# First batch's row products of the two halves in own PSUM banks, joined by VectorE; transfer lengths of the planner changed

## The chip, the cores and the metric

The kernel runs on one core of a Trainium2 chip. A core has five engines, each with its own instruction queue that is worked off strictly in order: TensorE (PE, matrix products into PSUM), VectorE (DVE), ScalarE (ACT), GpSimd (POOL) and SyncE (SP, here only a queue for transfers). 16 DMA engines move data between DRAM and SBUF for the queues of SP, ACT and POOL. The metric is the time of one execution in microseconds (us), as the device measures it; lower is better.

## The reference: what is computed

Two stages follow each other, for 4 batches of 768 positions. The first is attention in chunks: 8 heads of 64, each chunk of 32 positions sees 16 positions to the left, 8 to the right and 8 memory rows.

```python
for c in range(nc):                       # 24 chunks of 32
    k_full = np.concatenate([mem_k, k_ctx], axis=2)
    scores = scale * np.matmul(q_c, k_full.transpose(0, 1, 3, 2))
    a = softmax(scores)
    out[:, :, c_start:c_end] = np.matmul(a, v_full)
```

The result, as x of 4 x 768 x 512, goes through a Fourier mix and a two-layer network:

```python
X = np.fft.fft(np.fft.fft(x, axis=1), axis=2)
u = x + np.real(X)
un = (u - mean(u)) / np.sqrt(var(u) + 1e-06)
out = u + np.maximum(un @ w_ch1, 0.0) @ w_ch2      # 512 -> 2048 -> 512
```

## The kernel before

**Attention.** The 8 heads of a batch are taken in 4 pairs; over the whole run the pairs are numbered 0 to 15 (batch 0 has 0 to 3, batch 1 has 4 to 7). Per pair, `e_load_q` and `e_load_k` (L310, L315) issue a q and a k transfer on POOL, which also turn the numbers into bf16. `e_load_v` (L320) issues six transfers on SP into a buffer `va`; `e_overlap` (L339) copies on POOL, once per head, 32 rows of `va` to the rows where neighbouring chunks overlap. `e_turn_q`, `e_turn_k` transpose on PE, `e_qT` and `e_kT` copy the result out of PSUM, `e_scores` and `e_exp` make the weights for one half (group g) of the sequence, `e_values` (L430) multiplies them with `va` on PE, and `e_norm` (L443) divides on DVE. There are 4 buffers each for q and k, 3 for `va`.

**Fourier mix.** The real part of the two-dimensional transform is computed as cosine and sine products. The columns are folded first (`pq`, `ff`), so that sums and differences of mirrored columns remain. Each folded block is split into two fp16 parts, `hi` (ACT, L501) and `lo` (DVE, L506). The row products (`row_products`, L509) multiply these on PE with the tables `cosS` and `sinS` of the sequence axis, 12 matrix products of 128x193 for one result; a result is named by `par` (even or odd output columns) and `ab` (0 for cosine, 1 for sine). Each is split again into `up` (cast on ACT, L528) and its rest (DVE, L532), reversed into `dn` (DVE, L537), and goes as the left operand into the column products on PE.

**Batch 0 in its own form.** To begin before all of batch 0's attention is there, its columns are folded in two halves h = 0 (pairs 0 and 1) and h = 1 (pairs 2 and 3), with `e0_pq` (L554), `e0_ff` (L587) and `e0_ff_edge`. `e0_rows` (L597) accumulates both halves into the same four PSUM banks `ps0`, one for each (par, ab): first the four results of h = 0, later the four of h = 1 on top. Where par and ab differ, h = 1 enters with a minus sign, which a negated table gives (`e_neg`, L782, on DVE). `e0_edge` (L571) adds the products of one boundary column, 24 of one row, whose parts POOL prepares in `e0_edge_parts` (L562).

**The network.** `unT` (512 x 768 per batch, transposed, fp16) goes through the first layer (`e_ch1`, L666, 4 products of 128x384 per group, `relu` on ACT into `hT`) and the second (`e_ch2`, L679, from `hT`). The weights are fetched by POOL with conversion to fp16: `load_w1` (L889) and `load_w2` (L899), four transfers each. The buffer of w2 is the one that held v of pair 3 (`last`), so that w2 is issued after the values of pair 3.

**The order.** All of this is written as tasks with an engine, a cost, predecessors, buffers to take and give, and for transfers a length `moved`. `Plan.order` (L59) plays them through with these numbers and hands out the order in which each engine's instructions are written, and the PSUM bank of each result. The numbers are estimates in the source; only the order follows from them, and on the chip each engine waits where data is not there. `wire` in the planner sums the lengths of all transfers one behind the other:

```python
if t["moved"] and e == "POOL":
    beside = max(beside, now + cost) + 1.15 * t["moved"]
    wire = max(wire, now + cost) + t["moved"]
    t["done"] = beside + self.LAG["DMA"]
```

Where PE has nothing to do in the plan, filler products (`e_warm`, six at a time) are put in. POOL's transfers use eight semaphores in turn: each waits for the one eight before it on POOL to have landed.

The softmax here doesn't subtract the row's maximum and nothing guards it: scores larger than these inputs give would overflow.

## Time and profile before

| | us |
|---|---|
| median of 13 runs (304.32 to 309.48) | 305.77 |
| the profiled execution | 305.29 |
| its span, first to last instruction | 303.4 |
| PE busy | 290.1 (3333 products) |
| DVE busy | 179.5 |
| ACT busy | 166.1 |
| POOL busy | 72.4 |
| row products of batch 0, h = 1 (48 products) on PE | about 40.4 to 44.4 from the start |
| first product of the first layer | 54.9 from the start |

The busy time of an engine is the time in which one of its instructions runs; an idle stretch is followed in the trace by the instruction that ended it and by what released it (`<-`). The chain of waits is followed back from the last instruction to whatever released each step. In timelines, the first number is the start from the beginning of the span, the second the duration; `x12` means twelve instructions in one entry. SPq and POOLq are the queue parts of these engines. The granted clock of TensorE is 1.00 at full speed.

### The profile page before, as it was taken

What the parts mean: (1) busy time and instruction counts of PE and PEld (TensorE: products, weight loads), DVE (VectorE), ACT (ScalarE), POOL (GpSimd) and SP (SyncE); (2) the same over time, 40 slices, a digit from 0 to 9 for tenths busy, and PEclk for the clock granted to TensorE, in tenths of its full rate; (3) what the DMA queues carried; (4) which work ended last, traced back from release to release, by engine and by line L of the source; (5) the groups of instructions that cost most, each with busy time, mean ns of one, the idle gap of its engine ahead of it and who ended that gap; (6) DMA issues with size and microseconds to landing.
All of it is one profiled execution on the core that took longest, in us unless ns stands there. A gap on an engine that the chain in (4) does not pass through costs nothing.

```text
span 303.4 us, 7854 instructions
## 1 busy us (share of the span) xinstructions
PE 290.1 (96%) x3333; PEld 193.1 (64%) x3333; DVE 179.5 (59%) x362; ACT 166.1 (55%) x297; POOL 72.4 (24%) x121
## 2 busy tenths in 40 slices
PE   8798998899999999999899999999999999999995
PEld 8677997556556666767566856656764554554644
DVE  7988967903323999789997889865931001002002
ACT  8967546686467757367655454721680450630710
POOL 7557732633235822025400020000020000000000
PEclk9999999999999999999999999999999999999999
DMA  6999999995995513213200001001000101101001
GB/s 80 158 165 191 195 202 194 197 190 69 189 175 95 106 30 96 67 31 99 56 0 2 35 37 38 0 37 52 19 0 35 72 0 69 37 0 69 37 35 69
DMA packets 42313, 24.49 MB, mean 81 GB/s; under 512 B 30375, under 2 KB 38823, under 8 KB 42279
## 3 DMA queue, kind: packets, MB, share of 16 engines
q0 software_dynamic: 9344, 10.49, 22.2%
q1 hardware_dynamic: 29479, 7.34, 13.6%
q10 hardware_dynamic: 3456, 6.16, 5.4%
q8 instruction: 26, 0.43, 0.6%
q14 instruction: 8, 0.07, 0.1%
HBM read 28.11 MB, written 6.29 MB: 113 GB/s over the span
## 4 chain that ended last, share of the span: by engine, by line
PE 74%; DVE 11%; DMA 7%; ACT 4%; POOL 2%; issue 1%; ACTq 0%; POOLq 0%; SPq 0%
PE pc L683 25%; PE ph L669 24%; PE xa L439 6%; PE pm L548 5%; DMA w_sb<-in_moe_w_ch_dram 5%; PE ps L513 4%; PE sc L384 2%; PE tp L648 2%; PE trq L348 2%; DVE xsb L450 1%; PE trk L363 1%; ACT e L427 1%; DMA qf<-in_q_dram 1%; PE pc_half L691 1%; DVE ff L490 1%
## 5 line engine op out<-in xcount | busy, mean ns | idle before, releaser
L676 ACT ACTIVATE hT<-ph 128x384 f16<-128x384 f32 x128 | 61.7, 492 | 58.9 <-PE ph L669 58.0
L669 PE MATMUL ph<-unT,w_sb 128*128 128x384 f16 x512 | 88.9, 326 | 1.9 <-ACT hT L676 1.6
L683 PE MATMUL pc<-w_sb,hT 128*128 128x512 f16 x368 | 85.7, 380 | 0.2 <-DVE osb L711 0.2
L669 PEld LDWEIGHTS <-w_sb 128*128 128x128 f16 x512 | 48.5, 98 | 34.5 <-issue 3.1
L711 DVE SCALAR_TENSOR_TENSOR osb<-pc,rstd,xsb 128x512 f32<-128x512 f32 x23 | 17.3, 751 | 74.8 <-PE pc L683 74.8
L683 PEld LDWEIGHTS <-hT 128*128 128x128 f16 x368 | 34.0, 98 | 37.1 <-issue 0.2
L341 POOL COPY va<-va 32x780 f32<-32x780 f32 x30 | 31.3, 1065 | 32.7 <-DMA va<-in_v_dram 20.8
L392 ACT ACTIVATE e<-sc,mbias 128x384 f32<-128x384 f32 x48 | 25.3, 581 | 13.4 <-PE sc L384 7.3
L439 PE MATMUL xa<-va,e 128*64 128x65 f32 x720 | 26.4, 225 | 2.2 <-POOL va L341 2.2
L439 PEld LDWEIGHTS xa<-va,e 128*64 128x64 f32 x720 | 23.1, 137 | 7.7 <-issue 3.4
L642 ACT ACTIVATE un<-xsb,mu_s 128x512 f16<-128x512 f32 x18 | 12.9, 719 | 14.6 <-DVE mu_s L636 13.8
L660 POOL TENSOR_SCALAR rstd<-mu_s 128x6 f32<-128x6 f32 x4 | 1.0, 245 | 77.8 <-DVE mu_s L636 77.7
L528 ACT CAST up<-ps 128x386 f16<-128x386 f32 x16 | 9.7, 605 | 17.7 <-PE ps L513 17.6
L450 DVE TENSOR_TENSOR xsb<-xa,zs 128x384 f32<-128x384 f32 x32 | 17.8, 557 | 1.1
L635 DVE BATCH_NORM_STATS2 st<-xsb 128x6 f32<-128x512 f32 x24 | 16.6, 690 | 0.6
L373 ACT COPY kTb<-trk 128x832 bf16<-128x832 bf16 x16 | 13.5, 854 | 3.6 <-PE trk L363 3.6
L353 ACT COPY qT<-trq 128x768 bf16<-128x768 bf16 x14 | 11.2, 798 | 7.2 <-PE trq L348 4.0
L506 DVE TENSOR_TENSOR lo<-ff,hi 128x768 f16<-128x768 f32 x14 | 14.4, 1043 | 0.9 <-ACT hi L501 0.9
L312 POOL DMA_DIRECT2D qf<-in_q_dram x16 | 10.5, 659 | 17.1 <-PE trq L348 11.7
L449 DVE RECIPROCAL zs<-xa 128x6 f32<-128x6 f32 x32 | 6.0, 188 | 13.6 <-PE xa L439 13.2
L317 POOL DMA_DIRECT2D kf_all<-in_k_dram x16 | 10.1, 632 | 15.2 <-PE trk L363 5.2
L368 DVE COPY kTb<-mkT 128x96 bf16<-128x96 bf16 x16 | 5.8, 388 | 12.8 <-PE sc L384 12.8
(147 smaller groups left out, 416.0 us busy)
## 6 DMA issues: line engine op xcount, KB each, us to landing
out_dram<-osb ACTq DMA_DIRECT2D x23, 256.0 KB
va<-in_v_dram SPq DMA_DIRECT2D x30, 176.0 KB
w_sb<-in_moe_w_ch_dram POOLq DMA_DIRECT2D x8, 512.0 KB, 12.6
qf<-in_q_dram POOLq DMA_DIRECT2D x16, 192.0 KB, 4.8
kf_all<-in_k_dram POOLq DMA_DIRECT2D x16, 192.0 KB, 5.7
va<-in_mem_v_dram SPq DMA_DIRECT2D x30, 24.0 KB
va<-in_v_dram SPq DMA_DIRECT2D x15, 28.0 KB
last<-in_v_dram SPq DMA_DIRECT2D x2, 176.0 KB
```

The lines of the kernel that those rows point to most:

```text
L341: nc.gpsimd.tensor_copy(v1[0:32, 1:NB, 0:D + 1], v1[96:128, 0:NT, 0:D + 1])
L373: nc.scalar.copy(strided(kTb[n % NKT], 0, [[BS, NB], [8, 8], [1, RB]]), strided(tr_of.pop((n, 1)), 0, [[8, NB], [1, 8], [KP, RB]]))
L392: nc.scalar.activation(e1[:, :, :, ts(half, 32)], sc[:, :, 0:6, ts(half, 32)], AFT.Exp, bias=mbias[:, half:half + 1], scale=1.0 / math.sqr ...
L439: nc.tensor.matmul(xa[64 * half:64 * half + 64, st, hh, 0:65], e1[:, hh, t6, :], v1[:, 6 * g + t6 + 1, 0:65], start=True, stop=True)
L450: nc.vector.tensor_tensor(xs[b][:, 3 * g:3 * g + 3, 2 * pr * D:(2 * pr + 2) * D] .rearrange("p s (h d) -> p s h d", h=2), xa[:, :, :, 0:D] ...
L506: nc.vector.tensor_tensor(lo[:, ab].rearrange(fl), ff_of[b, par][:, ab].rearrange(fl), hi[:, ab].rearrange(fl), ALU.subtract)
L548: nc.tensor.matmul(pm[:, par, :], lhs, rhs[:, par, :], start=(im == 0), stop=(im == 3))
L635: nc.vector.bn_stats(st6, xs[b][:, kt, :])
L669: nc.tensor.matmul(ph[:, 0:384], w1_sb[:, dt, ts(ht, P)], unT_of[b][:, dt, sh * 384:(sh + 1) * 384], start=(dt == 0), stop=(dt == NDT - 1))
L676: nc.scalar.activation(hT_of[b, sh][:, ht, :], ph_of.pop((b, sh, ht))[:, 0:384], AFT.Relu, bias=0.0, scale=-1.0)
L683: nc.tensor.matmul(pc_of[b, sh, stl], hT_of[b, sh][:, ht, ts(stl, P)], w2_of[0][:, ht, :], start=(ht == 0), stop=(ht == NHT - 1))
L711: nc.vector.scalar_tensor_tensor(osb, pc_of.pop((b, sh, stl)), rstd_of[b][:, st:st + 1], xs[b][:, st, :], ALU.mult, ALU.add)
```

## The change

Batch 0's two halves no longer share PSUM banks. For h = 0, three results are formed, each in a bank of its own: one for the cosine (both parities have the same one) and one per parity for the sine, since the edge products, which now open their own accumulation in row 0, differ there. For h = 1, two results are formed. So 5 times 12 products stand where 8 times 12 stood, and the negated tables go. ACT copies the three results of h = 0 to SBUF in float32 (`e0_keep`); DVE adds or subtracts the result of h = 1 (`e0_join`), four times; the cast (`e0_up`) and the rest (`e0_rest`) then read SBUF. The order of two predecessors changes with it: the edge parts follow the first `pq` of h = 1, and the second norm of pair 2 follows the `ff` of h = 0.

The planner's lengths change: v of batches 1 to 3 counts 0.9 instead of 1.6, each part of w1 2.2 instead of 3.2, each part of w2 2.2 instead of 3.5.

```diff
@@ e0_edge
-            row_products(ps_of[0, par, 1][0:1],
-                         [e128[:, i].unsqueeze(3) for i in range(2)], par, tab, 0, 1,
-                         False, False)
+            row_products(ps_of["own", par, 1][0:1],
+                         [e128[:, i].unsqueeze(3) for i in range(2)], par, tab, 0, 1)
@@
-    def e0_rows(par, ab, h):
-        if h == 0:
-            ps_of[0, par, ab] = bank([P, 2, NK], FP32, "ps0")
-        ps = ps_of[0, par, ab]
-        turned = h == 1 and par != ab
-        tab = neg_of[0][:, ab] if turned else (cosS if ab == 0 else sinS)
-        row_products(ps, hl_of[0, h], ab, tab, 0, P, h == 0, h == 1)
+    def e0_rows(key, ab, h):
+        ps_of[key] = ps = bank([P, 2, NK], FP32, "ps0")
+        row_products(ps, hl_of[0, h], ab, cosS if ab == 0 else sinS, 0, P)
+    t_of = []
+    def e0_keep(key, ab):
+        if not t_of:
+            t_of.append(fpool.tile([P, 2, 2, 2, NK], FP32, tag="unT", bufs=2, name="join"))
+        nc.scalar.copy(t_of[0][:, ab, key[1]], ps_of.pop(key))
+    def e0_join(par, ab):
+        op = ALU.add if par == ab else ALU.subtract
+        nc.vector.tensor_tensor(t_of[0][:, ab, par], t_of[0][:, ab, ab and par],
+                                ps_of["other", ab], op)
+    def e0_up(par, ab):
+        up = fpool.tile([P, 2, NK, 2], FP16, tag="up", bufs=4, name="up")
+        up_of[0, par, ab] = [up.rearrange("p i k s -> p i (k s)"), None, up]
+        nc.scalar.copy(up[:, 0].rearrange("p k s -> p s k"), t_of[0][:, ab, par])
+    def e0_rest(par, ab):
+        up = up_of[0, par, ab][2]
+        nc.vector.tensor_tensor(up[:, 1].rearrange("p k s -> p s k"), t_of[0][:, ab, par],
+                                up[:, 0].rearrange("p k s -> p s k"), ALU.subtract)
@@
-    def e_neg(i):
...
-    t_neg = [add("DVE", 0.4, lambda i=i: e_neg(i), t_sines[:2], rank=140 + i,
-                 take=("unT",) if i == 0 else ()) for i in range(2)]
@@ attention
-                  take=("va",) if hh == 0 and n != HP - 1 else (), moved=1.6) for hh in range(2)]
+                  take=("va",) if hh == 0 and n != HP - 1 else (), moved=1.6 if n < HP else 0.9) for hh in range(2)]
...
-                 [t_mkT, kept.get("mk"), t_clear["kTb", n] if n < NKT else None], take=("kTb",),
+                 [t_mkT, kept.get("mk"), t_clear["kTb", n] if n < NKT else None,
+                  kept["f0"] if n == HP + 1 else None], take=("kTb",),
@@ load_w1, load_w2
-            w1_sb[:, dt, :], moe_w_ch1[ts(dt, P), :]), [after], moved=3.2, rank=-1)
+            w1_sb[:, dt, :], moe_w_ch1[ts(dt, P), :]), [after], moved=2.2, rank=-1)
-        return [add("POOL", 0.7, lambda g=g: e_w2(g), [after], moved=3.5, rank=-1)
+        return [add("POOL", 0.7, lambda g=g: e_w2(g), [after], moved=2.2, rank=-1)
@@ part_of_first
-                ed = add("POOL", 0.8, e0_edge_parts, [pq[-1]], rank=-3)
-                ed = add("PE", 1.94, e0_edge, [ed, rows[0, 1], rows[1, 1]])
+                ed = add("POOL", 0.8, e0_edge_parts, [pq[1]], rank=-3)
+                ed = add("PE", 1.94, e0_edge, [ed, rows["own", 0, 1], rows["own", 1, 1]])
+                for par in range(2):
+                    own = rows["own", par, 1]
+                    keep[par, 1] = add("ACT", 0.6, lambda par=par: e0_keep(("own", par, 1), 1),
+                                       [ed], give=(("acc", own),))
...
+                more = [kept["tk0"]] + t_sines if h == 0 else []
+                for par in range(2 if (h, ab) == (0, 1) else 1):
+                    key = ("own", par, ab) if h == 0 else ("other", ab)
...
+            if h == 0:
+                keep[0, 0] = add("ACT", 0.6, lambda: e0_keep(("own", 0, 0), 0), [rows["own", 0, 0]],
+                                 take=("unT",), give=(("acc", rows["own", 0, 0]),))
+                t_norm[2, 1]["after"].append(ff)
+        join = up = None
+        for ab in range(2):
+            other = rows["other", ab]
+            for par in (1 - ab, ab):
+                t_join[par, ab] = join = add(
+                    "DVE", 0.6, lambda par=par, ab=ab: e0_join(par, ab),
+                    [keep[ab and par, ab], other, join],
+                    give=(("acc", other),) if par == ab else ())
+        for ab in range(2):
+            for par in (1 - ab, ab):
+                up = add("ACT", 0.5, lambda par=par, ab=ab: e0_up(par, ab), [t_join[par, ab], up],
+                         take=("up",))
+                t_rest[par, ab] = add("DVE", 0.45, lambda par=par, ab=ab: e0_rest(par, ab), [up],
+                                      give=("unT",) if par and ab else ())
```

## The prediction

> **What bounds the kernel now.** I read the busy table first. All times are us from the start of the profiled span.

> ```profile
> PE 290.1 (96%) x3333; PEld 193.1 (64%) x3333; DVE 179.5 (59%) x362; ACT 166.1 (55%) x297; POOL 72.4 (24%) x121
> ```

> TensorE (PE) is busy for 96% of the span, so the end is set by how much real work PE has left once it runs without a break, and by when that stretch starts. Windows of 5 us show where the break is:

> ```profile
> 45.00:50.00 5.00, 5.00 (x59) 4.30 (x58) 3.97 (x13) 3.45 (x6) 0.76 (x2) 1.00 1.22 196
> 50.00:55.00 5.00, 3.21 (x82) 2.66 (x80) 4.39 (x15) 1.74 (x4) 3.11 (x5) 1.00 1.22 196
> 55.00:60.00 5.00, 4.45 (x51) 2.83 (x52) 4.76 (x15) 4.16 (x8) 2.27 (x4) 1.00 1.22 197
> ```

> The columns are PE, weight loads, VectorE (DVE), ScalarE (ACT), GpSimd (POOL), granted clock, DMA share, GB/s. PE stands 1.79 us in the second window while the DMA engines move 196 GB/s. The chain of waits over 30 to 62 us says why:

> ```profile
> 35.98 15.31 DMA w_sb<-in_moe_w_ch_dram
> ...
> 51.88 0.14 POOL kf_all L317
> 52.02 0.50 issue
> 52.52 1.62 POOL va L341 x2
> 54.14 0.04 issue
> 54.18 0.80 PE xa L439 x20
> ```

> Nothing that PE, DVE or ACT does between 36 and 51 us is on it. The second w2 transfer lands at 35.98 + 15.31 = 51.29; then POOL issues a k load, then copies the overlap rows of v for pair 4 (the first of batch 1), and PE's attention values of pair 4 wait for that copy. POOL's timeline shows the queue that ties them:

> ```profile
> 35.19 3.04 POOL L897 DMA_DIRECT2D w_sb<-in_moe_w_ch_dram  x4
> 38.18 0.69 POOL L312 DMA_DIRECT2D qf<-in_q_dram  x1
> ...
> 48.44 0.63 POOL L312 DMA_DIRECT2D qf<-in_q_dram  x1 [3.31 <-DMA w_sb<-in_moe_w_ch_dram]
> 51.85 0.63 POOL L317 DMA_DIRECT2D kf_all<-in_k_dram  x1 [2.78 <-DMA va<-in_v_dram]
> 52.52 3.17 POOL L341 COPY va<-va 32x780 f32<-32x780 f32 x4
> 55.65 0.63 POOL L312 DMA_DIRECT2D qf<-in_q_dram  x1
> 58.42 0.63 POOL L317 DMA_DIRECT2D kf_all<-in_k_dram  x1 [2.15 <-PE tp L648]
> ```

> In the program each POOL transfer waits for the semaphore of the eighth POOL transfer before it. Counting back eight, the q load at 48.44 waits for w2 part 0, the k load at 51.85 for part 1 (landed 51.29, 0.56 earlier), the q load at 55.65 for part 2, the k load at 58.42 for part 3. The transfer view has part 3 landing 20.4 us after its start:

> ```profile
> w_sb<-in_moe_w_ch_dram POOLq DMA_DIRECT2D x1, 512.0 KB, 20.4
> ```

> The four issues at 35.19 take 3.04, so part 3 starts at about 37.45 and lands at 57.85; again 0.57 passes before the POOL instruction at 58.42. So the release label that names `tp` on that line is not the cause; the landing is.

> **The change, part by part.**

> Moved, and the term that decides. With shorter lengths (w1 and w2 2.2 instead of 3.2 and 3.5, v 0.9 instead of 1.6) the planner writes another order. On POOL the q and k loads of pair 9 now stand ahead of the four overlap copies of pairs 4 and 5; before, they stood behind. They are the two that wait for w2 parts 2 and 3. The bytes, the rings and the issue order up to there are the same, and the DMA engines carry 196 to 198 GB/s through this stretch, so I let part 3 land at 57.85 as before. Then the copies start not at 52.52 but after the k load: 58.42 + 0.63 + 0.04 = 59.09, which is 6.57 later. The values of pair 4, group 0 ended at 54.98 and now end at 61.55. Behind the two waiting loads stand six overlap copies, a q and a k load and batch 0's `rstd`; behind the waiting values on PE stands everything to the end.

> PE's order also changed: ahead of these values it now has the scores of pair 5 (0.27), two first-layer groups (2 x 0.65, from 10.40 for 16) and one turn of `un` (0.33). That is 1.90 done in the wait: 6.57 - 1.90 = +4.67. In the old order PE ran from 54.98 to 59.53 with 4.55 us for three first-layer groups (1.95), one values group (0.71) and three turns (0.9), so 0.99 went to waits on ACT's `hT`. Behind a 5 us stand all this is ready, so I take it back whole: +3.68. Bounds: w2 up to 0.5 earlier (the edge parts that precede its issue on POOL may come 0.5 sooner) or 0.5 later; the 0.99 regained from nothing to all.

> Removed: 36 row products (60 + 24 against 96 + 24). Twelve take 1.01, so 3.03 of PE. The two negated tables, 0.45 + 1.09 of DVE at 14.8, lie beside DMA and ACT; the first norm waits no longer for DVE, but the second still waits for PE.

> Added: three ACT copies from PSUM (0.60 each, from the `up` cast of the same 386 columns), four DVE sums and differences (0.56 to 0.60, from `pq` and the old rest); four `up` casts and rests now read SBUF (bounds 0.45 to 0.60). Walked on these rows: The last norm of pair 2 moves behind `ff`, which makes the second half's low parts 0.75 later, and the last row product ends at 42.3 instead of 44.4. Joins then run to 43.7 on DVE, casts to 44.6 on ACT, rests to 45.9 on DVE. Two of the ACT copies wait for the edge products (39.75); behind them on ACT stand the copy of q for pair 5, the four casts and the next `exp`. Behind the joins on DVE stand the rests, the reversals and batch 0's sums. The first column product starts at 45.1 (before 44.48) behind two scores and turns and four fillers of 0.51, the columns end at 52.9 (before 50.5), and PE reaches the values of pair 4 at about 54.8. It meets a copy that ends at 59.92. So the whole row-product part is costed at nothing: 5.1 us of standing hides it. If that cover were gone, the values would end at 55.65 against 54.98 with 1.90 more done: 0.67 - 1.90 = -1.2.

> The v lengths move the later pairs' attention forward in the order. PE stands there little: 50 - 48.13 = 1.87 between 100 and 150 us and 0.55 between 150 and 200. So this part lies between -2.4 (all of it gone) and +2.4 (as much again); I take 0, since the same engines remain busy and DMA is at 69 GB/s or less.

> Sum: 305.29 (the profiled run: span 303.4 and 1.89 around it) + 3.7 = 309.0. That run lies 0.48 under the median of 305.77, so against the median: 309.4.

> [...] This trace's w2 parts land 51.29 and, two later, 57.85: 3.28 us each. [...]

> The clock: the page's rows grant 1.00 throughout, over standing times up to 1.79 us; no row here shows PE standing 5 us. [...]

> **The rivals.**

> Faster (0.11): w2 part 3 lands early enough that the copies are no obstacle. Against it: 3.28 us each at a saturated 196 GB/s. Price -1.2, so 304.6; it needs the landing 3.7 us sooner than 57.85, at 54.2, just to break even.

> Paid back later (0.10): the stand occurs, but attention moved forward fills the 2.42 us of later standing and some waits of ACT's `hT` (1.6 in the waits) go too: 3.7 - 2.4 - 1.0 = +0.3, about 306.1. For it: the order is denser in attention after 62 us. Against: those waits come from short dependences that any order has.

> A second stand (0.09): the overlap copy for pair 6 waits for v, which landed before 65.36 in the old trace; the loads of pair 10 stand behind it. If PE's values of pair 6 or the turns of pairs 7 and 8 caught up with that, as much again as 3.7 would be lost: 313.1. Against it: PE has some 15 us of other work between.

> The change does not shorten (a rival to the gain only): joins and rests take longer than the two rows saved, and the columns start late. This I expect, but it is hidden.

> **How the numbers follow.** The likeliest (0.70) is the stand, 309.4, with its own range 306.5 to 313.3 from -0.5 -2.4 and +0.5 +1.0 +2.4. Dropping the faster case below and the top of the second stand above leaves about 8 in 10 in 305.0 to 312.8. A measurement tells 0.2% (0.6 us) from no change. Faster: 0.11 and a third of the paid-back case, 0.14; within: a third of it and the low end of the likeliest, 0.06; slower: the rest, 0.80.

> **What would show it.** Right: the overlap copies of pair 4 start near 59 on POOL, behind two loads that wait for `w_sb`; PE waits about 5 us for `va` before the values at about 55; the row products number 84 + later batches, and the four joins run near 41.3 to 43.7. Also to be seen: whether the clock stays 1.00 after it. Wrong: the copies start before 55.5, or PE arrives at the values later than 59, or standing time after 100 us goes away by over 2 us.

## The result and the profile after

The changed kernel takes 310.38 us (median of 11 runs, 308.98 to 311.62), the kernel before 305.89 (48 runs, 304.24 to 309.62). The ratio is 1.0143, 95% interval 1.0119 to 1.0167: slower by about 4.4 us. The forecast was 309.4, slower.

| us | before | after |
|---|---|---|
| the profiled execution | 305.29 | 311.26 |
| its span | 303.4 | 309.3 |
| PE busy | 290.1 | 290.3 |
| PE not busy, 0 to 30 | 5.13 | 6.19 |
| PE not busy, 30 to 56 | 1.83 | 1.98 |
| PE not busy, 56 to 100 | 0.51 | 5.34 |
| PE not busy, 100 to 200 | 2.42 | 2.12 |

The span grew by 5.9, PE's idle time by 5.7 (19.0 against 13.3), and 4.83 of that lies between 56 and 100 us. The busy table of after and its windows of 5 us (columns as before) show the place:

```profile
PE 290.3 (94%) x3327; PEld 193.9 (63%) x3327; DVE 177.4 (57%) x364; ACT 167.7 (54%) x300; POOL 68.7 (22%) x121
```

```profile
50.00:55.00 5.00, 5.00 (x65) 4.30 (x63) 3.97 (x15) 2.99 (x5) 1.26 (x2) 1.00 1.22 197
55.00:60.00 5.00, 2.09 (x26) 1.24 (x24) 4.79 (x16) 4.19 (x8) 0.63 (x1) 1.00 1.23 199
60.00:65.00 5.00, 2.57 (x44) 2.41 (x46) 1.09 (x5) 0.04 (x1) 4.50 (x6) 0.72 1.23 201
```

PE is busy 2.09 and 2.57 of two times 5 us, and the DMA engines move 197 to 201 GB/s throughout. The third window also has a clock of 0.72, where the kernel before had 1.00. The chain of waits of after, 30 to 64 us, ends in the same links as before; the transfer at its head is now the last part of w2 (39.96 + 19.94 = 59.90), and the copies start 8.6 us later:

```profile
39.96 19.94 DMA w_sb<-in_moe_w_ch_dram
60.49 0.14 POOL kf_all L315
60.77 0.36 issue
61.13 1.62 POOL va L339 x2
62.79 1.24 PE xa L437 x17
```

POOL's timeline (start, duration, and in brackets the idle time ahead of it and its releaser) shows what now stands in front of the copies:

```profile
37.70 3.03 POOL L905 DMA_DIRECT2D w_sb<-in_moe_w_ch_dram  x4 [0.45 <-DMA va<-in_mem_v_dram]
...
50.28 0.63 POOL L310 DMA_DIRECT2D qf<-in_q_dram  x1 [3.10 <-DMA w_sb<-in_moe_w_ch_dram]
53.62 0.63 POOL L315 DMA_DIRECT2D kf_all<-in_k_dram  x1 [2.70 <-DMA w_sb<-in_moe_w_ch_dram]
57.00 0.63 POOL L310 DMA_DIRECT2D qf<-in_q_dram  x1 [2.75 <-PE ph L685]
60.46 0.63 POOL L315 DMA_DIRECT2D kf_all<-in_k_dram  x1 [2.82 <-DMA w_sb<-in_moe_w_ch_dram]
61.13 4.74 POOL L339 COPY va<-va 32x780 f32<-32x780 f32 x6
```

The first two loads are those of pair 8, the next two those of pair 9. Each waits for one part of w2, 3.3 to 3.5 us apart (the label `ph` on the third is only the last other event, as `tp` was before); the copies stand behind the fourth where they stood behind the second. PE's timeline shows the price:

```profile
56.70 0.39 PE L664 MATMUL tp<-ident_h,un 128*128 128x128 f16 x4
62.01 0.36 PE L437 MATMUL xa<-va,e 128*64 128x65 f32 x4 [4.92 <-POOL va L339]
62.79 2.65 PE L437 MATMUL xa<-va,e 128*64 128x65 f32 x44 [0.42 <-POOL va L339]
```

PE stands 4.92 us before the values of pair 4; each of their two groups (the two halves of the sequence) has 24 products, and the entries x4 and x44 hold both. PE's busy time did not fall although 36 row products went (3.03 by the forecast): the planner put in 30 fillers more (3327 products against 3333 before), and fillers are 15.3 us busy against 12.3. The new operations ran as the diff says, on DVE and ACT, well ahead of it:

```profile
45.03 2.10 DVE L608 TENSOR_TENSOR join<-join,ps 128x386 f32<-128x386 f32 x4 [1.51 <-PE ps L511]
47.05 2.02 DVE L618 TENSOR_TENSOR up<-join,up 128x386 f16<-128x386 f32 x4
```

```profile
42.99 0.95 ACT L604 COPY join<-ps 128x386 f32<-128x386 f32 x2
45.63 2.22 ACT L614 CAST up<-join 128x386 f16<-128x386 f32 x4 [0.85 <-DVE join L608]
```

The first column product follows at 48.06. So what is to be explained is a POOL queue order, not arithmetic. Two things changed at once that can move that order: the form of the row products with its predecessors ("rows"), and the planner's lengths ("lengths"). The prediction's theory: the shorter lengths put the loads of pair 9 ahead of the copies. The rival: the new rows did it, since the planner is free to place everything again when tasks change. Filler products, where an experiment adds them, write into a PSUM tile that the real products then overwrite.

### The profile page after: what moved, and what is told of

The parts are those of the page before. It is cut to its first block, busy times and chain, and to the rows that moved or that the text cites. A ratio compares the mean times of both kernels' runs of the same rounds, so it can differ in the third digit from the quotient of the medians.

```text
span 309.3 us, 7849 instructions
## 1 busy us (share of the span) xinstructions
PE 290.3 (94%) x3327; PEld 193.9 (63%) x3327; DVE 177.4 (57%) x364; ACT 167.7 (54%) x300; POOL 68.7 (22%) x121
## 4 chain that ended last, share of the span: by engine, by line
PE 73%; DMA 12%; DVE 9%; POOL 2%; issue 2%; ACT 1%; SPq 0%; POOLq 0%
PE ph L685 26%; PE pc L699 23%; DMA w_sb<-in_moe_w_ch_dram 6%; PE xa L437 6%; PE pm L546 5%; PE ps L511 4%; DMA va<-in_v_dram 2%; DMA kf_all<-in_k_dram 2%; PE warm L460 2%; DVE lo L504 2%; PE sc L382 1%; PE trk L361 1%; DVE ff L488 1%; PE tp L664 1%; PE trq L346 1%
## 5 line engine op out<-in xcount | busy, mean ns | idle before, releaser
L699 PE MATMUL pc<-w_sb,hT 128*128 128x512 f16 x368 | 84.8, 379 | 0.6 <-DVE unT L670 0.6
L339 POOL COPY va<-va 32x780 f32<-32x780 f32 x30 | 28.0, 954 | 38.4 <-PE trq L346 22.7
L437 PE MATMUL xa<-va,e 128*64 128x65 f32 x720 | 27.9, 231 | 7.0 <-POOL va L339 5.3
L437 PEld LDWEIGHTS xa<-va,e 128*64 128x64 f32 x720 | 24.4, 143 | 12.2 <-POOL va L339 6.1
L499 ACT CAST hi<-ff 128x768 f16<-128x768 f32 x14 | 11.4, 830 | 9.3 <-DVE ff L488 7.8
L460 PE MATMUL warm<-zeros 128*128 128x128 bf16 x182 | 15.3, 251 | 1.0 <-DVE zero L247 1.0
L645 DVE TENSOR_TENSOR xsb<-pm,xsb 128x512 f32<-128x512 f32 x18 | 12.1, 673 | 5.2 <-PE pm L546 5.2
L460 PEld LDWEIGHTS <-zeros 128*128 128x128 bf16 x182 | 13.3, 115 | 1.6 <-DVE zero L247 1.0
## 6 DMA issues: line engine op xcount, KB each, us to landing
w_sb<-in_moe_w_ch_dram POOLq DMA_DIRECT2D x8, 512.0 KB, 12.5
```

The source lines that it names most:

```text
L339: nc.gpsimd.tensor_copy(v1[0:32, 1:NB, 0:D + 1], v1[96:128, 0:NT, 0:D + 1])
L437: nc.tensor.matmul(xa[64 * half:64 * half + 64, st, hh, 0:65], e1[:, hh, t6, :], v1[:, 6 * g + t6 + 1, 0:65], start=True, stop=True)
L460: nc.tensor.matmul(warm_of[0], zeros, zeros, start=True, stop=True)
L699: nc.tensor.matmul(pc_of[b, sh, stl], hT_of[b, sh][:, ht, ts(stl, P)], w2_of[0][:, ht, :], start=(ht == 0), stop=(ht == NHT - 1))
```

## Experiments

Ratios are to the kernel before, run beside each group of experiments on the same chip: its median was 307.51 (17 runs) beside the parts alone, pair 9's loads behind, and the 56 fillers; 306.14 (23 runs) beside the four kernels with the copies ahead of pair 8's loads; 305.87 (11 runs) beside the 84 fillers, the unchanged kernel and the fillers at the start. Times of different groups are compared by these ratios.

### One part at a time

**Old rows, new lengths.**

```diff
--- the kernel before
-    moved=1.6                      # v
+    moved=1.6 if n < HP else 0.9
-    moved=3.2 ... moved=3.5        # w1, w2
+    moved=2.2 ... moved=2.2
```

> The rows as before, the shorter transfer lengths of the change. Theory 1 (the prediction's attribution: the lengths put the loads of pair 9 ahead of the overlap copies of pair 4): PE stands about 5 us and the time is near 310. Theory 2 (the new form of the rows does it, because PE then turns q and k of pair 5 earlier, and with that their buffers come free earlier in the plan): the copies stand ahead of these two loads, start near 52.5 as before, PE stands under 2 us, and the time is 305 to 307; in this kernel's written order the copies do stand ahead.

Measured: 306.55 us, ratio 1.0007 [0.9969, 1.0044]. POOL's timeline:

```profile
51.77 0.63 POOL L317 DMA_DIRECT2D kf_all<-in_k_dram  x1 [2.91 <-PE tp L648]
52.45 3.18 POOL L341 COPY va<-va 32x780 f32<-32x780 f32 x4
55.58 0.63 POOL L312 DMA_DIRECT2D qf<-in_q_dram  x1
```

The copies start at 52.45 (before: 52.52) and the loads of pair 9 follow them, as theory 2 expected. The lengths do not move them: the theory of the prediction falls here.

**New rows, old lengths.**

```diff
--- the kernel after
-    moved=1.6 if n < HP else 0.9
+    moved=1.6
-    moved=2.2 ... moved=2.2        # w1, w2
+    moved=3.2 ... moved=3.5
```

> The rows of the change, the transfer lengths of before. Theory 1: no stand, about 304.6. Theory 2: the loads of pair 9 stand ahead of the copies as in the changed kernel, the copies start near 59 to 61, PE stands about 5 us, and the time is 309 to 312.

Measured: 317.83 us, ratio 1.0329 [1.0278, 1.0379]. POOL's timeline, then PE's:

```profile
59.57 0.63 POOL L315 DMA_DIRECT2D kf_all<-in_k_dram  x1 [2.68 <-DMA w_sb<-in_moe_w_ch_dram]
60.24 3.97 POOL L339 COPY va<-va 32x780 f32<-32x780 f32 x5
```

```profile
61.12 0.48 PE L437 MATMUL xa<-va,e 128*64 128x65 f32 x4 [8.08 <-POOL va L339]
```

The new rows alone bring the bad order, as theory 2 expected, but the time lies above the expected 309 to 312. The longer stand, 8.08 us, is not the reason: in this execution PE arrived earlier (53.04 against 57.09 in after), and the values of pair 4 start 0.9 earlier than in after (61.12 against 62.01). What makes it slower than after comes behind them, 254.5 us to the end of the span against 247.3: PE is not busy for 5.77 of the stretch from 100 to 200 us, against 2.12 in after, and is busy 293.2 in all against 290.3. So the lengths do not set the order of these loads, but with the new rows and the planner's order they take 1.0329 down to 1.0143; which tasks do this was not traced.

Why the rows move POOL's loads can be read in PE's timeline and in the planner's list. A q load of pair 9 needs one of four buffers, the one that pair 5 gives back when PE has turned it. The kernel before, at pair 5:

```profile
50.88 0.35 PE L384 MATMUL sc<-qT,kTb 64*128 64x64 bf16 x12
51.15 0.53 PE L348 MATMUL trq<-ident_b,qf 96*64 96x96 bf16 x16
51.52 0.54 PE L363 MATMUL trk<-ident_b,kf_all 104*64 104x104 bf16 x16
53.40 0.34 PE L439 MATMUL xa<-va,e 128*64 128x65 f32 x4 [1.35 <-POOL va L341]
```

And after:

```profile
43.35 0.53 PE L346 MATMUL trq<-ident_b,qf 96*64 96x96 bf16 x16
...
45.94 0.35 PE L382 MATMUL sc<-qT,kTb 64*128 64x64 bf16 x12
46.22 0.56 PE L361 MATMUL trk<-ident_b,kf_all 104*64 104x104 bf16 x16
```

With the new rows the turns of pair 5 are written between the row products, 5 to 8 us earlier on the chip. In the planner's own list, pair 5's q turn stands at 39.0 on its time scale with the new rows, with either set of lengths, and at 50.6 with the old rows, with either set; the first overlap copy of pair 4 stands at 48 to 50. So with the new rows the buffer is free in the plan before POOL reaches the copies, and the planner places the loads of pair 9 ahead of them. In its list each such load takes 0.8 on POOL; the wait for the eighth transfer before it, 2.7 us and more on the chip, does not appear there. Which piece of the new rows lets the turn move (fewer products, the banks, or the changed predecessors) was not separated.

### The order alone

**After, with the loads of pair 9 behind the copies of pair 5.**

```diff
--- the kernel after, in attention(n)
-                   HP + 2: t_w2[-1] if n >= HP else None}.get(n)
+                   HP + 2: t_w2[-1] if n >= HP else None,
+                   HP + 5: kept.get(("ov", HP + 1))}.get(n)
```

> The changed kernel, with one predecessor more in the plan: the q load of pair 9 follows the second overlap copy of pair 5. If the two loads ahead of the copies cause the loss, the copies start some 6.5 us sooner, the long stand of PE goes, the clock stays at 1.00 in that place, and the time is 304 to 306 (4 to 6 below 310.4). If the late column products (joins, casts and rests) cause it, the time stays within 1 of 310.4.

Measured: 303.09 us, ratio 0.9868 [0.9823, 0.9913]; span 300.1, clock 1.00. POOL, then PE:

```profile
48.69 0.63 POOL L310 DMA_DIRECT2D qf<-in_q_dram  x1 [2.78 <-PE tp L664]
52.08 0.63 POOL L315 DMA_DIRECT2D kf_all<-in_k_dram  x1 [2.75 <-DMA va<-in_v_dram]
52.75 3.18 POOL L339 COPY va<-va 32x780 f32<-32x780 f32 x4
```

```profile
53.63 0.34 PE L437 MATMUL xa<-va,e 128*64 128x65 f32 x4 [2.53 <-POOL va L339]
54.41 1.50 PE L437 MATMUL xa<-va,e 128*64 128x65 f32 x44 [0.45 <-POOL va L339]
```

One line of order turns 1.4% slower into 1.3% faster; the time lies below the 304 to 306 expected. The span is 9.2 us shorter than in after, and 8.4 of that lies ahead of the first values of pair 4 (53.63 against 62.01; w2 was also issued earlier in this execution, at 33.97 against 37.70). Without the two loads ahead of the copies the whole loss is gone and the change is a gain. The line also lets the planner place later tasks anew, and a part of the gain comes from there: from 100 to 200 us PE is not busy for 0.47, against 2.12 in after.

**The same one load pair further ahead, for all four combinations.** Here the loads of pair 8 too are put behind the copies of pairs 4 and 5 (`HP + 4: kept.get(("ov", HP + 1))` in place of the `HP + 5` line), so that no copy waits for w2.

> The kernel before, with the q and k loads of pair 8 (and so of pair 9) after the overlap copies of pairs 4 and 5 on POOL. Theory 2 (the copies are held up by loads that wait for w2, in the kernel before as well, by two loads fewer): the copies start near 46 to 49, the stand of 1.79 before the values of pair 4 goes, and the time is 303.5 to 305.5. If the stand were set by something else, 306 as before.

> Rows of the change, lengths of before, loads of pair 8 and 9 after the copies. Theory 2: the 8.1 stand of the same kernel without this order goes, 317.8 falls by 8 to 14. Whether the new rows alone are then faster than the old ones is the row products' own worth: 0.5 to 3 below the old rows with old lengths in the same order if the 3.0 of removed products counts; level or above if joins and rests eat it.

> The changed kernel with the loads of pairs 8 and 9 after the copies. With only those of pair 9 behind, PE still stood 2.53 and 0.45 for the copies at 53.6. Theory 2: that goes too, the copies start near 46 to 49, and the time is 299.5 to 302.

> Old rows, lengths of the change, loads of pair 8 after the copies. With the stand gone this and the three kernels beside it tell rows and lengths apart: the lengths alone gain 0 to 2 against old rows with old lengths, the rows 0.5 to 3 against this one; 302.5 to 305.5.

Measured, as ratios to the kernel before, with the planner's own order beside it:

| | planner's order | copies ahead of pair 8's loads |
|---|---|---|
| old rows, old lengths | 1 | 0.9956 [0.9922, 0.9991], 304.72 us |
| old rows, new lengths | 1.0007 [0.9969, 1.0044] | 0.9974 [0.9942, 1.0006], 305.75 us |
| new rows, old lengths | 1.0329 [1.0278, 1.0379] | 0.9861 [0.9800, 0.9921], 301.47 us |
| new rows, new lengths | 1.0143 [1.0119, 1.0167] | 0.9869 [0.9824, 0.9915], 301.94 us |

POOL's timeline of the fastest, new rows with old lengths, and its values on PE:

```profile
45.30 1.16 POOL L315 DMA_DIRECT2D kf_all<-in_k_dram  x1 [2.06 <-DMA w_sb<-in_moe_w_ch_dram]
46.50 2.52 POOL L339 COPY va<-va 32x780 f32<-32x780 f32 x3
```

```profile
51.57 1.62 PE L437 MATMUL xa<-va,e 128*64 128x65 f32 x48
```

No wait stands before the values. Two of these times lie just outside what was expected: by the ratios, new rows with old lengths fell by 14.3 (expected 8 to 14), and old rows with new lengths took 305.75 (expected at most 305.5). In the right column, where the copies are out of the way, new rows against old are worth 0.0095 (old lengths) and 0.0105 (new lengths) of about 306 us: 2.9 and 3.2 us, each uncertain by about 2. PE's busy time agrees: 287.7 with new rows against 290.5 with old (old lengths) and 288.5 against 290.9 (new lengths), 2.8 and 2.4 less, with the 30 fillers more counted in (the 290.5 holds a low clock at the start that the 287.7 does not; both of the second pair hold it); the 36 products that went were put at 3.03. The lengths bring nothing that can be seen in that column: 0.9956 against 0.9974, 0.9861 against 0.9869, each difference inside the intervals. Moving the copies ahead is worth 0.4% with the old rows and 2.7% with the changed kernel.

### What the stand does to the clock

In after the granted clock falls behind the stand. Windows of 1 us:

```profile
62.00:63.00 1.00, 0.57 (x8) 0.41 (x10) 0.00 (x0) 0.00 (x0) 1.00 (x2) 0.59 1.24 202
63.00:64.00 1.00, 1.00 (x22) 1.00 (x22) 0.00 (x0) 0.00 (x0) 1.00 (x2) 0.50 1.23 201
64.00:65.00 1.00, 1.00 (x24) 1.00 (x22) 0.78 (x3) 0.00 (x0) 1.00 (x2) 0.50 1.24 205
65.00:66.00 1.00, 1.00 (x14) 0.61 (x11) 0.93 (x4) 0.00 (x0) 0.87 (x2) 0.70 1.17 193
```

To price it, filler products were put into the stand, so that PE works through it while the copies stay as late: first 56, then 84 (with the unchanged kernel measured beside the 84).

```diff
--- the kernel after, in e_values(n, g)
+        if (n, g) == (HP, 0):
+            for _ in range(56):     # 84 in the second
+                nc.tensor.matmul(xa.rearrange("p s h c -> p (s h c)")[:, 0:P],
+                                 zeros, zeros, start=True, stop=True)
```

> The changed kernel, with 56 filler products of 128x128 on PE ahead of the values of pair 4, where PE stands 4.92 us in the profile; at 84 ns each they take 4.7 us at full clock. If the halved clock after the stand costs time, it stays at 1.00 from 62 to 66 and the time falls by 1.2 to 1.8 below 310.4. If the clock there costs nothing, the time is the same or up to 0.5 more.

> The changed kernel itself, to be compared on the same chip with the two beside it: 310.4 as before, within 1; the stand before the values of pair 4 about 5 us.

> The changed kernel with 84 fillers ahead of the values of pair 4, which at the measured 59 ns each take 4.9 us. If the halved clock after the stand costs what the profiles say (from the first of these values to the end 247.3 without and 246.1 with fillers), the time is 0.8 to 1.6 below the changed kernel beside it, with the clock at 1.00 after the stand. If it costs nothing in the end, the two are level.

Measured: 56 fillers 310.85 us, ratio 1.0122 [1.0071, 1.0172], a stand of 2.76 left; 84 fillers 310.01, ratio 1.0128 [1.0094, 1.0163]; the unchanged kernel beside it 310.52, ratio 1.0149 [1.0122, 1.0176]. The 56 had been sized at 84 ns each and took 59. By the ratios the time fell by 0.6 us both times, less than expected (1.2 to 1.8, then 0.8 to 1.6). PE and the window behind the copies with 84 fillers:

```profile
56.33 4.85 PE L434 MATMUL xa<-zeros 128*128 128x128 bf16 x84
61.40 0.34 PE L441 MATMUL xa<-va,e 128*64 128x65 f32 x4 [0.21 <-POOL va L339]
62.18 1.50 PE L441 MATMUL xa<-va,e 128*64 128x65 f32 x44 [0.45 <-POOL va L339]
```

```profile
60.00:65.00 5.00, 4.34 (x90) 3.60 (x89) 1.86 (x6) 0.52 (x2) 4.96 (x7) 1.00 1.25 205
```

And the unchanged kernel beside it:

```profile
61.56 0.49 PE L437 MATMUL xa<-va,e 128*64 128x65 f32 x4 [5.44 <-POOL va L339]
```

```profile
60.00:65.00 5.00, 3.14 (x49) 2.83 (x50) 1.22 (x3) 0.00 (x0) 4.60 (x6) 0.50 1.23 199
```

That the stand takes the clock down is shown: 1.00 with the stand filled, 0.50 without. At that place it costs 1.15 us: the 44 products of the values last 2.65 in after and 1.50 with 84 fillers. What is left of this at the end is not resolved. From the first values to the end of the span it is 247.3 (after) against 246.1 (56 fillers, the fastest of its six executions), and 246.9 against 246.7 in the pair on one chip; the medians of that pair differ by 0.5 us, and the intervals of their ratios allow anything from nothing to about 2 us.

### A stand at the start

The profile of after has another low clock, 0.66 between 10 and 15 us, behind 2.46 us in which PE waits for the first k load; several other kernels show it too. So 30 fillers were put into that wait in the fastest kernel.

```diff
--- new rows, old lengths, copies ahead; in e_turn_k(n)
+        if n == 0:
+            e_warm(30)
```

> New rows, old lengths, copies ahead (301.47), with 30 fillers more in PE's wait for the first k load, where PE stands 1.7 to 3.1 us in the profiles and the clock then falls to 0.66 in 10 to 15 us in six of ten of them. If that dip costs time, the clock stays at 1.00 there and the time is 300 to 301; if it is absorbed by later waits of the first batch, 301.5, as without.

Measured: 301.8 us, ratio 0.9889 [0.9842, 0.9936], against 0.9861 without. The clock is 1.00 there and nothing is gained. That profile of the kernel without the fillers had 1.00 there as well, so this says that the fillers do not help, not what the dip costs where it occurs.

## Why the prediction was right, and where it was wrong

**The chain and its mechanism: right.** The pair 9 loads stand ahead of the copies, wait for w2 parts 2 and 3, and PE stands before the values of pair 4: 5.1 us forecast, 4.92 measured. The dependence on the eighth transfer before it held in every run: whoever has the loads in front starts the copies at 59.7 to 61.1 (after 61.13, new rows alone 60.24), whoever has not at 46 to 53.

**"With shorter lengths the planner writes another order": wrong.** This is the failed step. The lengths alone leave the order and the time (1.0007); the new rows alone write the new order (8.08 us of standing, 1.0329). The two planned orders of before and after had been compared with both parts changed, and the order was put down to the part that is about the planner. What did it is that the new rows let PE turn pair 5 earlier, which frees its buffer. The number did not suffer, because the forecast took the order as it is written in the changed kernel and did not derive it from the lengths.

**The size: +3.7 of standing, right within about 1 us.** The median moved by 4.5 (310.38 against 305.89; the ratio's interval gives 3.6 to 5.1), the profiled run by 5.97. In the profiles the two sides of the sum can be read apart. The values of pair 4 begin 8.61 later (62.01 against 53.40), where 6.57 was forecast; from there to the end of the span it is 247.3 against 250.0, 2.7 less, where 1.90 + 0.99 = 2.89 less was forecast, though this stretch also holds the half clock and all that changed in the later pairs. (The 0.99 taken back is more than there was: from 55 to 60 us PE is not busy for 0.55 in the kernel before.) In the second profile of after (under "What the stand does to the clock") the two are 8.16 later and 3.1 less. So the term that was too small is the landing of w2's last part, taken as unchanged at 57.85: it landed at 59.90. Its load followed at 60.46, and at 59.07 to 60.01 in the other four kernels or profiles with this order, against 58.42 before. A late start of this one execution explains only a part: w2 was issued at 37.70 (forecast: as before, 35.19), but in the new rows alone it was issued at 34.13 and that load still came at 59.57. That the stand itself came out so near (4.92 for 5.1) was luck: PE's arrival (57.1 against 54.8) and the copies (61.13 against 59.09) were both late by about 2. Where PE was less late or early, the same order gave stands of 5.44 and 8.08.

**Row products costed at nothing: right for this kernel; "if that cover were gone, -1.2": too small.** With pair 9's loads behind the copies the measured change is -1.3%, 4.0 us [2.7, 5.4]. Its span is 3.3 shorter than that of the kernel before: PE is busy 2.7 less (287.4 against 290.1) and idle 0.6 less (12.7 against 13.3; 1.95 less from 100 to 200 us, 1.45 more before 56). So what the -1.2 left out is mostly work that PE no longer has and that only counts once the wait is gone. The walk behind it, new rows reaching the end of the first values group 0.67 later (55.65) with 1.90 more done, can't be read off this kernel, where PE still waits for the copies and the planner placed that work behind the values. Where nothing waits (copies ahead, old lengths), the new rows reach the first values at 51.57 and the old ones at 52.48, and have 246.7 and 250.0 us left: not later but 0.9 earlier, in one profile each (that of the old rows has the low clock at the start).

**Later pairs, taken as 0 within 2.4 either way:** in after the standing from 100 to 200 us fell by 0.30. "Paid back later" did not happen, nor did a second stand: PE waits for copies 5.3 us in all, and that is the 4.92 and the 0.42 of pair 4. With other orders the same stretch moved by -1.95 (pair 9's loads behind) and +3.35 (new rows with old lengths), so the bounds were too narrow to hold for all orders, though they held for this one.

**The clock, left out of the sum:** no row of the kernel before shows PE standing 5 us. The windows of the runs show what followed: 3.4 us at half clock with the stand of 4.92, 6.8 with that of 5.44 and 10.3 with that of 8.08. Of its cost 1.15 us can be seen in the values of pair 4 (2.65 against 1.50 with the stand filled), and 0.5, within the noise, between the times with the stand filled and unfilled.

**The transfers:** the forecast read 3.28 us per w2 part in the trace of before, and in after POOL's issues that wait for these parts are 3.3 to 3.5 us apart. The "faster" rival needed the last part at 54.2 just to break even; it landed at 59.90.

## What to carry to other kernels

A change to the arithmetic of one stage also changes what a planner can place when, and the order of an in-order queue that no one edited can then cost more than the arithmetic brings; compare the queues' orders before and after, and undo each part alone before saying which one moved them. Work that releases the critical engine (here, 3.2 us of copies on POOL) should not stand in a queue behind transfers whose issue waits for earlier large transfers: one added predecessor moved this kernel from 1.4% slower to 1.3% faster than the kernel before. A wait hides gains as well as costs: what the edit to the rows is worth showed only with the wait taken out.

## What the runs showed of the hardware that was not expected

The length of PE's gap does not decide alone whether the clock falls. At the start PE waits for the first k load; after waits of 1.80 (second profile of after), 2.03 (84 fillers), 2.46 (after) and 3.08 (old rows, new lengths) the clock was 0.66 between 10 and 15 us, after 1.74 (before), 2.03 (pair 9's loads behind) and 2.33 (new rows, old lengths, copies ahead) it was 1.00; 0.66 occurs in eight of the twelve profiles without fillers at that place. In mid-run, stands of 2.53 and 2.76 left it at 1.00. In the second profile of after even two stands of 0.68 and 0.76, less than 3 us apart, were followed by 0.50 from 32 us on:

```profile
30.00:31.00 1.00, 0.41 (x6) 0.32 (x6) 1.00 (x2) 0.94 (x2) 0.08 (x1) 1.00 1.29 206
31.00:32.00 1.00, 0.83 (x15) 0.64 (x14) 0.69 (x2) 0.83 (x2) 0.99 (x2) 0.79 1.35 163
32.00:33.00 1.00, 1.00 (x12) 0.81 (x12) 1.00 (x2) 0.90 (x2) 1.00 (x3) 0.50 0.69 98
```

Nor does the fall come at a fixed time after the stand begins: in the first profile of after the stand began at 57.09 and the clock fell at about 62, in the second it began at 56.12 and the clock fell at about 59, while PE still stood. But within each of these two profiles the falls lie whole multiples of one length apart. The trace shows 1.00 and 0.50 and means between them; taken as a mix of the two, a mean of 0.59 from 62 to 63 puts the fall at 62.18, and the windows from 62 to 66 hold 3.4 us at half. The fall at the start of the same profile is at 10.98 (0.99 from 10 to 11), 51.20 earlier, which is 15 times 3.413. In the second profile the falls at 31.58 (0.79 from 31 to 32) and 58.88 (0.94 from 58 to 59) are 27.30 apart, 8 times 3.413. The window of the first fall in after, and that of the second in its second profile:

```profile
10.00:11.00 1.00, 0.82 (x22) 0.76 (x23) 0.86 (x4) 1.00 (x3) 0.40 (x5) 0.99 1.02 136
```

```profile
58.00:59.00 1.00, 0.00 (x0) 0.00 (x0) 0.96 (x3) 1.00 (x3) 0.00 (x0) 0.94 1.20 192
```

Filler products of 128x128 follow each other at 58 to 59 ns (56 in 3.29, 84 in 4.85). A group of six lasts 0.51 in the trace, but the next product starts 0.35 after it (38.78 and 39.13 in after): the two entries overlap by 0.16. The walk counted four groups at 0.51 each; the 24 take 1.35 to the next start (46.71 to 48.06). No term of the sum rests on it.
